# The first two batches' local softmax by head on ScalarE, the weights' pieces in six buffers, and a new hand-written order

## The chip, the cores and the metric

The kernel runs on one core of one Trainium2 chip. A core has five engines, each with an instruction queue of its own that is worked off in order: TensorE (PE in the profile, PEld its weight loads), VectorE (DVE), ScalarE (ACT), GpSimd (POOL) and SyncE (SP), which here only issues DMAs. The metric is the device time of one run in microseconds (us), the median of several runs. A profile is one execution taken apart instruction by instruction.

## The reference, cut to what matters

```python
# q, k, v: (B=8, H=8, S=576, D=64)
q_d, k_d, v_d = (mean of 4 neighbouring positions of q, k, v)       # 144 positions
out_d = softmax(q_d @ k_d.T / 8) @ v_d                             # "pooled" attention
out_up = repeat(out_d, 4, axis=position)
scores = where(|i - j| < 4, q @ k.T / 8, -1e9)                     # "local" attention
scores = scores - max(scores)
attn = exp(scores); attn = attn / (sum(attn) + 1e-9)
x = (out_up + attn @ v), as (4608 tokens, 512)
h = x @ w_in                                                       # (512, 1024)
e = exp(h - max(h)); solu = h * e / (sum(e) + 1e-9)
ln = (solu - mean) / sqrt(var + 1e-6) * g_ln
out = ln @ w_out                                                   # (1024, 512)
```

The weights `w_in` and `w_out` come as 64-bit floats, and the kernel makes 32-bit ones of them with integer operations.

## The kernel before, in words

**Attention, batch by batch.** A batch (`b` = 0 to 7) has 8 heads in 4 pairs (`pr`). For batches 0 to 2 TensorE transposes q and k (`qp_b_pr`, `kp_b_pr`, six transposes each), ScalarE copies them out of PSUM into `qT` and `kT`, and VectorE adds four neighbours each (`qd_flat`, `kd`). The pooled attention of a pair is `Pooled.steps`: scores `sd_b_pr` on PE, a maximum on DVE (`mxd`), three exponentials with their sums on ACT (`pd`, `smd`), a division on POOL, transposes `pdt` on PE, two copies `pdT` on ACT, and the product with the pooled values `vd` on PE (`po_b_pr`). The pooled values of batches 0 and 1 are made on PE (`pv_b_0`, `pv_b_1`) from the five value tiles `vw_b_u` and a matrix `sums`.

The local attention goes in five units (`u` = 0 to 4) of two windows of 64 positions each, `Local.by_tensor`: 16 small products give the scores `sc_b_u` of all heads; DVE adds the mask into `pl` (128 partitions by 4 pairs by 2 by 64) and takes each head's maximum `mxl`; POOL subtracts it; one ACT instruction takes the exponential of all 512 columns; DVE adds up each head (`sml`) and takes the reciprocal `rsl`; POOL multiplies; PE transposes (`plt_b_u`), ACT copies (`plT`), and 16 products with `vw` give `xp_b_u`, which is added to `x_b`. `pl` has four buffers, used in turn by unit number 5b + u.

**The feed-forward part** goes in 36 tiles of 128 tokens. `xhl(i)` splits x into two parts (`xh` on ACT, `xl` on POOL); `ffn_in` does 24 products of 128x512 into `h_i` and then the maximum `nmx` (DVE), `e` = exp (ACT), h times e (DVE), the mean's subtraction (ACT) and the squares' sum (ACT); `e` goes to DRAM as `u` and comes back as `v` (`ffn_back`), is transposed on DVE and split into `uh` (ACT) and `ul` (POOL); `ffn_out` does 24 products in two halves (first half columns 0 to 511 of the 1024, hence pieces 8 to 11 of the weights; second half pieces 12 to 15) into `o_i`.

**The weights** come in 16 pieces, 0 to 7 of `w_in`, 8 to 15 of `w_out`. `Weights.load(n)` loads piece n as 64-bit numbers, `Weights.f32` and `Weights.piece` make a 32-bit tile `w` of it and split it: one ACT instruction (L373), four on DVE (L375, L379, L384, L388), one or two on ACT (L407 for `w_out`, L409), one on POOL (L411). All eight pieces of `w_in` are needed before the first tile's products, all of `w_out` before the second half of `o_0`.

**The order** of all this is written out. `plan` collects the steps in program order, and `ORDER`, a string of 2072 numbers, gives the order in which they are issued; each engine keeps that order. `FILL` names PSUM tiles ahead of which PE does a number of products of the identity with itself (`idle_...`, L235), whose results nobody reads. A DMA that waits (for a buffer, or for the DMA eight before it) holds every DMA behind it in SP's queue.

Of the kernel before, what the change touches and what calls it, by code (L numbers as in the profile page):

```python
# [137 lines left out]
def pooled_local_attention_then_solu_ffn(  # L138
# [450 lines left out]

    ON_TENSOR = 8

    class Local:
# [514 lines left out]
```

## Time and profile before

| | |
|---|---|
| time, median of 3 runs | 617.78 us (616.66 to 618.25) |
| profiled execution | 620.24 us; span from first to last instruction 618.5 us |
| granted TensorE clock | 0.983 on average |
| busy | PE 597.7, DVE 394.0, ACT 374.1, POOL 374.6 us |
| DMA | 91.96 MB, 149 GB/s on average |
| longest chain | PE 81% of the span |

The span is the part of the time in which instructions ran; 1.7 us lie around it. PE's busy time holds the `idle_...` products too. From about 125 us on PE is busy without a gap worth speaking of; before that the batches 0 and 1, the weights and the first four tiles share the engines, and none of them is always busy.

### The profile page before, as it was taken

To read this page: it belongs to the slowest core of one execution; us is meant where nothing else is said; L and a number is where in the kernel's file an instruction comes from. 1 tells how busy PE (TensorE), PEld (TensorE's weight loads), DVE (VectorE), ACT (ScalarE), POOL (GpSimd) and SP (SyncE) were. 2 spreads that over 40 slices of the span, in tenths; PEclk is the share of its full clock that TensorE was granted. 3 is DMA by queue.
4 is the path that set the end of the run, shared out by engine and by line. 5 is a ranking of instruction groups with operands and counts; after the bars stand their busy time and mean duration, and the time that the engine had idled before them with its cause. 6 is when DMAs were issued, how large, how long until landed. Compare 5 with 4: busy or idle time off the path is not lost.

```text
span 618.5 us, 15210 instructions
## 1 busy us (share of the span) xinstructions
PE 597.7 (97%) x5912; PEld 470.4 (76%) x5912; DVE 394.0 (64%) x687; ACT 374.1 (60%) x810; POOL 374.6 (61%) x566
## 2 busy tenths in 40 slices
PE   5799998999999999999999999999999999999997
PEld 4686766878777777777777877777777777788876
DVE  4888897896646793668537873778367344443541
ACT  3647867965755576557755585557654675454451
POOL 7455485788735984499635983698556963332220
PEclk9698998999999999999999999999999999999999
DMA  9998966998795479535884398715532222234220
GB/s 179 216 208 204 186 163 183 182 163 195 187 204 149 133 191 193 153 115 159 185 179 131 109 192 195 198 43 164 164 115 81 92 87 86 86 107 147 86 103 34
DMA packets 205607, 91.96 MB, mean 149 GB/s; under 512 B 169568, under 2 KB 194400, under 8 KB 205536
## 3 DMA queue, kind: packets, MB, share of 16 engines
q1 hardware_dynamic: 205536, 91.00, 60.2%
q8 instruction: 46, 0.75, 0.5%
q14 instruction: 25, 0.20, 0.1%
HBM read 63.18 MB, written 27.79 MB: 147 GB/s over the span
## 4 chain that ended last, share of the span: by engine, by line
PE 81%; DVE 5%; ACT 5%; DMA 4%; SPq 3%; issue 1%; POOL 1%; ACTq 0%; DVEq 0%
PE o L965 32%; PE h L846 30%; PE xp L746 3%; PE plt L736 3%; PE po L828 3%; PE sc L696 3%; PE sd L772 2%; PE pdt L807 2%; DMA km<-in_k_dram 1%; SPq L550 1%; PE pv L488 1%; DMA w<-in_moe_w_in_dram 1%; SPq L314 1%; DVE pl L708 1%; ACT pd L787 1%
## 5 line engine op out<-in xcount | busy, mean ns | idle before, releaser
L846 PE MATMUL h<-wi_h,xh 128*128 128x512 f32 x288 | 117.4, 408 | 0.0
L965 PE MATMUL o<-wo_h,uh 128*128 128x512 f32 x288 | 117.0, 406 | 0.1
L965 PE MATMUL o<-wo_l,uh 128*128 128x512 f32 x288 | 114.2, 396 | 0.0
L846 PE MATMUL h<-wi_l,xh 128*128 128x512 f32 x288 | 114.1, 396 | 0.0
L846 PE MATMUL h<-wi_h,xl 128*128 128x512 f32 x288 | 114.0, 396 | 0.0
L951 POOL TENSOR_TENSOR ul<-v,uh 128x512 fp32r<-128x512 f32 x58 | 74.4, 1288 | 20.2 <-ACT uh L949 17.1
L854 DVE TENSOR_REDUCE nmx<-h 128x1 f32<-128x1024 f32 x36 | 43.7, 1215 | 61.9 <-PE h L846 61.9
L965 PE MATMUL o<-wo_h,ul 128*128 128x512 f32 x288 | 79.0, 396 | 0.0
L846 PEld LDWEIGHTS h<-wi_h,xh 128*128 128x128 f32 x288 | 54.2, 188 | 13.4 <-issue 0.4
L965 PEld LDWEIGHTS o<-wo_h,ul 128*128 128x128 f32 x288 | 54.2, 188 | 13.4
L965 PEld LDWEIGHTS o<-wo_h,uh 128*128 128x128 f32 x288 | 54.3, 189 | 13.3 <-ACT osb L972 0.3
L846 PEld LDWEIGHTS h<-wi_h,xl 128*128 128x128 f32 x288 | 54.2, 188 | 13.2
L846 PEld LDWEIGHTS h<-wi_l,xh 128*128 128x128 f32 x288 | 54.3, 189 | 11.6
L965 PEld LDWEIGHTS o<-wo_l,uh 128*128 128x128 f32 x288 | 54.2, 188 | 11.7
L999 POOL TENSOR_TENSOR xl<-x,xh 128x512 fp32r<-128x512 f32 (+1 forms) x40 | 47.3, 1191 | 25.2 <-ACT xh L996 25.1
L715 POOL TENSOR_TENSOR pl<-pl,mxl 128x512 f32<-128x512 f32 x40 | 42.8, 1075 | 26.7 <-DVE mxl L713 22.5
L858 ACT ACTIVATE e<-h,nmx 128x1024 f32<-128x1024 f32 x36 | 40.1, 1115 | 27.8 <-DVE nmx L854 27.5
L883 ACT ACTIVATE e<-e,nmu 128x1024 f32<-128x1024 f32 x35 | 40.2, 1149 | 25.2 <-POOL nmu L866 25.1
L943 DVE STREAM_TRANSPOSE v<-v 128x512 f32<-128x512 f32 x70 | 46.8, 693 | 12.8 <-DMA v<-u 12.5
L996 ACT ACTIVATE xh<-x 128x512 fp32r<-128x512 f32 (+1 forms) x40 | 22.7, 583 | 45.7 <-PE h L846 40.0
L949 ACT ACTIVATE uh<-v 128x512 fp32r<-128x512 f32 x70 | 43.3, 622 | 11.6 <-DVE v L943 5.7
L861 DVE SCALAR_TENSOR_TENSOR e<-h,e 128x1024 f32<-128x1024 f32 x36 | 43.5, 1210 | 10.2 <-ACT e L858 10.1
(121 smaller groups left out, 1150.3 us busy)
## 6 DMA issues: line engine op xcount, KB each, us to landing
u<-e SPq DMA_DIRECT2D x35, 512.0 KB
v<-u SPq DMA_DIRECT2D x140, 128.0 KB
vw<-in_v_dram SPq DMA_DIRECT2D x160, 64.0 KB
out_dram<-osb SPq DMA_DIRECT2D x36, 256.0 KB
vs<-in_v_dram SPq DMA_DIRECT2D x24, 288.0 KB
qm<-in_q_dram SPq DMA_DIRECT2D x20, 288.0 KB
km<-in_k_dram SPq DMA_DIRECT2D x20, 288.0 KB
w<-in_moe_w_out_dram SPq DMA_DIRECT2D x8, 512.0 KB
```

The lines of the kernel that those rows point to most:

```text
L715: nc.gpsimd.tensor_tensor(out=pl, in0=pl, in1=max_bc, op=ALU.subtract)
L846: nc.tensor.matmul(hps[:, n, :], src[:, cc, :], wt[:, cc, n * 512:(n + 1) * 512], start=(cc == 0 and src is xh and wt is wi_h), stop=(cc = ...
L854: nc.vector.tensor_reduce(out=nmx, in_=hf, op=ALU.max, axis=AX.X, negate=True)
L858: nc.scalar.activation(e, hf, AF.Exp, bias=nmx, scale=1.0, accum_out=se)
L861: nc.vector.scalar_tensor_tensor(out=e, in0=hf, scalar=1.0, in1=e, op0=ALU.mult, op1=ALU.mult, accum_out=su)
L883: nc.scalar.activation(e, e, AF.Identity, bias=nmu, scale=1.0)
L943: nc.vector.transpose(vg, vg)
L949: nc.scalar.activation(uh, tp, AF.Copy)
L951: (nc.vector if v is None or i in LATE else nc.gpsimd).tensor_tensor(out=ul, in0=tp, in1=uh.bitcast(F32), op=ALU.subtract)
L965: nc.tensor.matmul(o, src[:, j, :], wt[:, 4 * g + j, :], start=(g == 0 and j == 0 and src is uh and wt is wo_h), stop=(g == 1 and j == 3 a ...
L996: nc.scalar.activation(h, src, AF.Copy)
L999: nc.gpsimd.tensor_tensor(out=l, in0=src, in1=h.bitcast(F32), op=ALU.subtract)
```

## The change

Four things are edited. For batches 0 and 1 (`BY_HEAD = 2`) a local unit's exponential is no longer one ACT instruction behind a subtraction on POOL and ahead of a sum on DVE: DVE takes the negative maximum and scales it, and ACT does eight exponentials of 64 columns, one for each head, each with the head's maximum as bias and with its sum as a second output; DVE then adds 1e-9 to the eight sums. The raw 64-bit pieces 4, 5, 10 and 11 lie in the two buffers of `e` instead of in `big`; the 32-bit piece lies in turn in the buffers of `osb`, `uh` and `ul`, two each, instead of in the two of `osb`. `FILL` has other numbers (123 instead of 100 in all), and `ORDER` is another order of 2062 steps.

```diff
 FILL = {
-    "qp_0_3": (13, "o"), "pv_0_1": (8, "o"), "pdt_0_0": (3, "o"), "pdt_0_1": (1, "o"),
-    "sd_0_3": (2, "o"), "po_0_3": (3, "o"), "sc_0_0": (5, "o"), "plt_0_0": (12, "o"),
-    "xp_0_0": (2, "o"), "sc_0_1": (10, "o"), "h_0": (7, "o"), "qp_1_2": (3, "o"),
-    "po_1_3": (3, "h"), "kp_2_0": (5, "o"), "xp_2_0": (15, "h"), "o_34": (3, "h"),
-    "o_35": (5, "h"),
+    "qp_0_2": (4, "o"), "kp_0_2": (7, "o"), "qp_0_3": (3, "o"), "pv_0_0": (9, "o"),
+    "pv_0_1": (11, "o"), "po_0_0": (6, "o"), "sd_0_1": (4, "o"), "sc_0_0": (3, "o"),
+    "plt_0_0": (9, "o"), "sc_0_2": (17, "o"), "kp_1_1": (4, "o"), "sc_1_0": (8, "o"),
+    "sc_1_4": (2, "o"), "xp_1_4": (3, "o"), "qp_2_0": (5, "o"), "qp_2_2": (3, "o"),
+    "sc_2_1": (15, "h"), "o_34": (5, "h"), "o_35": (5, "h"),
 }
 ORDER = """
-0 33 7 14 1 2 3 28 8 4 5 6 9 10 135 40 11 12 29 13 15 41 42 50 143 16 43 51 44 151 136 52 137 45
...
+0 33 7 130 1 138 2 3 14 8 4 5 6 146 9 10 131 40 21 11 132 12 41 139 133 13 42 134 50 140 154 43
...
             elif n in (2, 3, 8, 9):
                 hl = moe.tile([P, DFF], F32, tag="v", name=f"w64_{n}", bufs=2)
+            elif n in (4,5,10,11):
+                hl = moe.tile([P, DFF], F32, tag="e", name=f"w64_{n}")
             else:
                 hl = big(f"w64_{n}")
...
-            t = moe.tile([P, DO], F32, tag="osb", name=f"w32_{n}", bufs=2)
+            t = moe.tile([P, DO], F32, tag=("osb", "uh", "ul")[n % 3], name=f"w32_{n}", bufs=2)
...
+    BY_HEAD = 2
...
+            if b < BY_HEAD:
+                nc.vector.tensor_reduce(out=mx, in_=pl, op=ALU.max, axis=AX.X, negate=True)
+                nc.vector.tensor_scalar(out=mx, in0=mx, scalar1=SCALE, scalar2=None, op0=ALU.mult)
+                yield
+                sm = small.tile([P, NPR, 2], F32, tag="sml", name=f"sml_{b}_{u}")
+                for pr in range(NPR):
+                    for a in range(2):
+                        nc.scalar.activation(
+                            pl[:, pr, a], pl[:, pr, a], AF.Exp, bias=mx[:, pr, a:a + 1], scale=SCALE,
+                            accum_out=sm[:, pr, a:a + 1],
+                        )
+                yield
+                nc.vector.tensor_scalar(out=sm, in0=sm, scalar1=1e-9, scalar2=None, op0=ALU.add)
+                rs = small.tile([P, NPR, 2], F32, tag="rsl", name=f"rsl_{b}_{u}")
+                nc.vector.reciprocal(out=rs, in_=sm)
+                yield
+            else:
...
-            row(it.steps(), 10 if isinstance(it, Pooled) else 11)
+            row(it.steps(), 10 if isinstance(it, Pooled) or bt.b < BY_HEAD else 11)
```

What the new order does is seen in the engines' queues. In the rows below the first number behind a name is the batch (or the piece, or the tile), the second the pair or unit, and the last a buffer's running number.

SP's queue near the start, before: `qm` and `km` are q and k, `w64` and `stage` the weights' pieces, `vw` the value tiles.

```order
L550 DMA km_0_125<-in_k_dram 96x6x64 x2
L314 DMA vw_0_0_188<-in_v_dram 64x4x64 x4
L360 DMA stage_211<-in_moe_w_in_dram 64x1024 x2
L314 DMA vw_0_1_223<-in_v_dram 64x4x64 x4
L360 DMA stage_211<-in_moe_w_in_dram 64x1024 x2
L360 DMA w64_2_260<-in_moe_w_in_dram 64x1024 x2
L360 DMA w64_3_291<-in_moe_w_in_dram 64x1024 x2
L360 DMA w64_4_304<-in_moe_w_in_dram 64x1024 x2
L550 DMA qm_0_3_313<-in_q_dram 96x6x64 x2
L550 DMA km_0_3_316<-in_k_dram 96x6x64 x2
L550 DMA qm_1_355<-in_q_dram 96x18x64 x2
L550 DMA km_1_356<-in_k_dram 96x18x64 x2
```

The same queue after:

```order
L362 DMA stage_166<-in_moe_w_in_dram 64x1024 x4
L552 DMA qm_0_124<-in_q_dram 96x6x64 x2
L552 DMA km_0_125<-in_k_dram 96x6x64 x2
L362 DMA w64_2_203<-in_moe_w_in_dram 64x1024 x2
L552 DMA qm_0_3_223<-in_q_dram 96x6x64 x2
L552 DMA km_0_3_226<-in_k_dram 96x6x64 x2
L362 DMA w64_3_259<-in_moe_w_in_dram 64x1024 x2
L362 DMA w64_4_287<-in_moe_w_in_dram 64x1024 x2
L314 DMA vw_0_0_314<-in_v_dram 64x4x64 x4
L314 DMA vw_0_1_369<-in_v_dram 64x4x64 x4
L314 DMA vw_0_2_442<-in_v_dram 64x4x64 x4
```

Pair 3's q and k of batch 0 now come behind three pieces of weights (0, 1 and 2) and no value tile, where they came behind five pieces and two value tiles; all five value tiles (`vw_0_3` and `vw_0_4` are the next rows) come ahead of batch 1's q and k, where three of them came behind these and behind pieces 5 to 7.

PE's queue ahead of the first tile's products, before:

```order
L746 MATMUL xp_0_0_937<-plT_0_0_615,vw_0_0_188 64x58 x16
L746 MATMUL xp_0_1_958<-plT_0_1_735,vw_0_1_223 64x58 x16
L736 MATMUL plt_0_2_978<-ident_82,pl_2_105 128x128 x4
L807 MATMUL pdt_1_0_991<-ident_82,pd_1_0_745 72x64 x12
L772 MATMUL sd_1_2_1008<-kd_1_619,qd_flat_111 64x144 x6
L736 MATMUL plt_0_3_1019<-ident_82,pl_3_106 128x128 x4
L235 MATMUL idle_h_0_1040<-ident_82 128x128 x7
L846 MATMUL h_0_1048<-wi_h_113,xh_0_1015 128x512
```

And after:

```order
L767 MATMUL xp_0_2_953<-plT_0_2_934,vw_0_2_442 64x58 x16
L570 MATMUL qp_1_3_981<-ident_82,qm_1_3_711 128x96 x6
L757 MATMUL plt_0_4_994<-ident_82,pl_0_103 128x128 x4
L570 MATMUL kp_1_3_1000<-ident_82,km_1_3_714 128x96 x6
L767 MATMUL xp_0_3_1011<-plT_0_3_988,vw_0_3_460 64x58 x16
L699 MATMUL sc_1_1_1033<-kT_1_779,qT_1_778 64x64 x16
L235 MATMUL idle_sc_1_0_1062<-ident_82 128x128 x8
L699 MATMUL sc_1_0_1071<-kT_1_779,qT_1_778 64x64 x16
L793 MATMUL sd_1_0_1088<-kd_1_780,qd_flat_111 64x144 x6
L867 MATMUL h_0_1097<-wi_h_113,xh_0_971 128x512
```

Before the first tile starts, batch 0's local units 0 to 3 are now done to the end (only `xp_0_4` is left) and batch 1's transposes of q and k come late, just ahead of it; before, units 2 to 4 were open and batch 1's pooled pairs further on.

ScalarE's queue there, after (a unit's eight exponentials are one row with x8):

```order
L411 ACTIVATE wi_h_113<-w32_7_900 128x4x4x32
L375 ACTIVATE w32_11_1059<-w64_11_822 128x512
L724 ACTIVATE pl_2_105,sml_1_1_1112<-pl_2_105,mxl_1_1_1055 128x64 x8
L804 ACTIVATE mxd_1_0_1110<-mxd_1_0_1110 128x3
L808 ACTIVATE pd_1_0_1131,smd_1_0_1132<-sd_1_0_1088,mxd_1_0_1110 128x144 x3
L812 ACTIVATE smd_1_0_1132<-smd_1_0_1132 128x3
L724 ACTIVATE pl_1_104,sml_1_0_1174<-pl_1_104,mxl_1_0_1122 128x64 x8
```

`wi_h` from piece 7, the last of `w_in`, stands there ahead of batch 1's first exponentials; five pieces of `w_out` have had their first step (L375) by then and wait for the rest.

From `h_4` on PE's queue is the same in both kernels, row for row but for the `idle_...` ones, and ahead of `h_4` PE does the same products in both, in another order.

More of the change, by code (lines that the diff above doesn't have):

```diff
@@ L712, in by_tensor @@
             yield
-            nc.vector.tensor_reduce(out=mx, in_=pl, op=ALU.max, axis=AX.X)
-            yield
-            nc.gpsimd.tensor_tensor(out=pl, in0=pl, in1=max_bc, op=ALU.subtract)
-            yield
-            nc.scalar.activation(by_pair, by_pair, AF.Exp, scale=SCALE)
-            yield
-            sm = small.tile([P, NPR, 2], F32, tag="sml", name=f"sml_{b}_{u}")
-            nc.vector.tensor_reduce(
-                out=sm, in_=pl_all.rearrange("p (r a w) -> p r a w", r=NPR, a=2), op=ALU.add, axis=AX.X
-            )
-            rs = small.tile([P, NPR, 2], F32, tag="rsl", name=f"rsl_{b}_{u}")
-            nc.vector.reciprocal(out=rs, in_=sm)
-            yield
+            if b < BY_HEAD:
[15 more added lines that the diff above has]
+            else:
+                nc.vector.tensor_reduce(out=mx, in_=pl, op=ALU.max, axis=AX.X)
+                yield
+                nc.gpsimd.tensor_tensor(out=pl, in0=pl, in1=max_bc, op=ALU.subtract)
+                yield
+                nc.scalar.activation(by_pair, by_pair, AF.Exp, scale=SCALE)
+                yield
+                sm = small.tile([P, NPR, 2], F32, tag="sml", name=f"sml_{b}_{u}")
+                nc.vector.tensor_reduce(
+                    out=sm, in_=pl_all.rearrange("p (r a w) -> p r a w", r=NPR, a=2), op=ALU.add, axis=AX.X
+                )
+                rs = small.tile([P, NPR, 2], F32, tag="rsl", name=f"rsl_{b}_{u}")
+                nc.vector.reciprocal(out=rs, in_=sm)
+                yield
             nc.gpsimd.tensor_tensor(
```

192 rows, old and new, of the table ORDER are left out of this document.

## The prediction

> **What bounds the kernel now.** I read the busy time by stage first, cut where the first tile's products start, where the first output tile `o_0` starts, and near `h_4` (the columns: stretch, its length, busy us of PE, PEld, DVE, ACT, POOL, granted clock, DMA share, GB/s), and then what lies in the early stages at 15 us each.
>
> ```profile
> 0.00:24.00 24.00, 15.41 (x113) 12.19 (x114) 13.63 (x29) 12.28 (x32) 14.30 (x43) 0.85 1.00 197
> 24.00:72.50 48.50, 44.17 (x615) 36.81 (x613) 41.88 (x71) 31.81 (x80) 26.88 (x23) 0.90 1.03 207
> 72.50:124.40 51.90, 49.27 (x694) 37.69 (x692) 44.76 (x72) 39.83 (x74) 33.71 (x43) 0.97 0.74 172
> 124.40:147.10 22.70, 22.70 (x285) 18.62 (x282) 16.19 (x31) 12.95 (x29) 19.82 (x24) 1.00 0.86 169
> 147.10:618.50 471.40, 466.11 (x4217) 365.09 (x4215) 277.55 (x488) 277.27 (x597) 279.84 (x436) 1.00 0.52 137
> ```
>
> ```profile
> 60.00:75.00 15.00, 14.59 (x243) 11.85 (x242) 13.32 (x21) 14.50 (x40) 8.85 (x8) 1.00 0.96 170
> 105.00:120.00 15.00, 14.93 (x192) 12.80 (x191) 13.09 (x24) 14.22 (x27) 10.60 (x15) 1.00 0.80 174
> ```
>
> From 147.1 us PE is busy 466.11 of 471.40 us and bounds the kernel. Since PE's rows from `h_4` on are the same after the change, the question is only when `h_4` starts. Ahead of it PE's busy time is partly the identity products, so I asked for line L235 alone (columns: stretch, length, PE, PEld, clock, DMA share, GB/s), then for PE in order of time.
>
> ```profile
> 0.00:72.50 72.50, 21.86 (x138) 20.06 (x138) 0.88 1.02 203
> 72.50:124.40 51.90, 1.58 (x13) 1.28 (x11) 0.97 0.74 172
> 124.40:147.10 22.70, 4.55 (x36) 4.17 (x36) 1.00 0.86 169
> ```
>
> ```profile
> 30.20 0.85 PE L568 MATMUL kp<-ident,km 96*128 96x96 f32 x6 [2.03 <-DMA km<-in_k_dram]
> ...
> 33.16 1.98 PE L696 MATMUL sc<-kT,qT 64*64 64x64 f32 x96
> ...
> 61.25 0.71 PE L828 MATMUL po<-pdT,vd 72*64 72x144 f32 x8 [0.27 <-DVE vd L502]
> ...
> 72.53 0.48 PE L846 MATMUL h<-wi_h,xh 128*128 128x512 f32 x1
> 72.84 0.40 PE L846 MATMUL h<-wi_l,xh 128*128 128x512 f32 x1
> 73.08 0.40 PE L846 MATMUL h<-wi_h,xl 128*128 128x512 f32 x1
> ...
> 124.37 0.50 PE L965 MATMUL o<-wo_h,uh 128*128 128x512 f32 x1
> ...
> 141.81 3.62 PE L235 MATMUL idle_xp<-ident 128*128 128x128 f32 x30
> ...
> 146.87 0.48 PE L846 MATMUL h<-wi_h,xh 128*128 128x512 f32 x1
> ```
>
> `h_4` starts at 146.87. Up to there PE idles 8.59 + 4.33 + 2.63 = 15.55 us (length less busy) and spends 21.86 + 1.58 + 4.55 = 27.99 us on identity products, so 146.87 - 15.55 - 27.99 = 103.3 us are work that the change leaves as it is. Those 43.5 us are all that there is to win. They come from three things: data that land late (the DMA engines are full, share 1.00 and 1.03, up to the first tile), the chain of batch 0 through the values, and the weights' pieces on ACT and DVE.
>
> **The change part by part.** *Loads.* The last transposes of batch 0, `kp_0_3`, wait for k until 30.20. What lies ahead in SP's queue is counted in KB of the DMAs:
>
> ```profile
> vw<-in_v_dram SPq DMA_DIRECT2D x46, 64.0 KB
> stage<-in_moe_w_in_dram SPq DMA_DIRECT2D x8, 256.0 KB
> w<-in_moe_w_in_dram SPq DMA_DIRECT2D x8, 256.0 KB
> qm<-in_q_dram SPq DMA_DIRECT2D x12, 144.0 KB
> km<-in_k_dram SPq DMA_DIRECT2D x12, 144.0 KB
> ...
> 39.91 9.12 SPq L314 DMA_DIRECT2D vw<-in_v_dram  x12
> ```
>
> Before: 16 of q and k (2304 KB), 10 of weights (2560), 8 of values (512), 5376 KB. After: 2304 + 6 of weights (1536) = 3840. The 1536 KB less (1.57 MB) are 7.8 us at about 202 GB/s: k lands at 22.4. The last values were issued at 39.91 + 9.12 = 49.0; now 3840 + 1024 + 1280 = 6144 KB (6.29 MB) must pass: 31 us, with 2.5 at the start some 34. Batch 1's q and k land later, about 44, and nobody is ready for them sooner. So the scores start at about 24.5 instead of 33.16.
>
> *Exponentials.* ACT's nearest rows are the pooled ones, 144 columns with a sum, and the unit's exponential that goes away (its shape's group):
>
> ```profile
> 12.20 0.38 ACT L787 ACTIVATE pd<-sd,mxd 128x144 f32<-128x144 f32 x1
> 12.48 0.19 ACT L787 ACTIVATION_READ_ACCUMULATOR pd<-sd,mxd 128x1 f32 x1
> 12.57 0.37 ACT L787 ACTIVATE pd<-sd,mxd 128x144 f32<-128x144 f32 x1
> ...
> L858 ACT ACTIVATE e<-h,nmx 128x1024 f32<-128x1024 f32 x4 | 4.4, 1108 | 0.0
> L717 ACT ACTIVATE pl<-pl 128x512 f32<-128x512 f32 x10 | 6.1, 622 | 2.2 <-POOL pl L715 2.2
> ```
>
> One starts 0.37 after the last, sum included. For 64 columns I take 0.29, since 80 columns less are 0.08 at the 0.95 ns a column between 512 columns (0.622) and 1024 (1.108); bounds 0.19 (the sum's row alone) and 0.37. Eight are 2.3 us, against 0.52 for the old one (0.62 less the 0.10 by which the next may start earlier, 12.48 for 12.20 + 0.38): +1.8 a unit, +17.8 for ten (10 to 24). The Trainium skill, page "ScalarE: Activation LUTs", section "Rules for kernel authors", budgets about 0.3 us for each ACTIVATE and 0.83 ns a column. By that eight would take an estimated 2.8 us, and batch 1's five units 1.5 us more than my sum has, the result 614.5 instead. The trace is against it: 144 columns would take 0.42 by the page, and start 0.37 apart.
>
> What leaves the other engines, and what the piece's first step waited for:
>
> ```profile
> L720 DVE TENSOR_REDUCE sml<-pl 128x8 f32<-128x520 f32 x10 | 6.8, 677 | 0.2 <-ACT pl L717 0.2
> L375 DVE TENSOR_SCALAR w<-w 128x512 f32<-128x512 f32 x16 | 11.1, 694 | 4.6 <-ACT w L373 4.6
> L724 DVE RECIPROCAL rsl<-sml 128x8 f32<-128x8 f32 x10 | 2.0, 203 | 0.9 <-POOL pl L715 0.5
> L715 POOL TENSOR_TENSOR pl<-pl,mxl 128x512 f32<-128x512 f32 x10 | 11.5, 1163 | 10.4 <-DVE mxl L713 10.4
> L373 ACT ACTIVATE w<-w 128x512 f32<-128x512 f32 x12 | 8.1, 677 | 1.1 <-DMA w<-in_moe_w_in_dram 0.7 <-POOL wi_l L411 0.3
> ACT w L407 <- DVE w L388: 6.1, 4, 3.9
> ```
>
> DVE loses ten sums (about 6 us) and gains twenty tiny ones of the reciprocals' shape (0.1 to 0.2 each): -3 (-2 to -4). POOL loses 11.5 us, and waited more than that, so it is worth nothing by itself; DVE's piece instructions may run a little sooner beside a quieter POOL (0 to 2 us of DVE, 0 taken). A unit's own chain is no shorter: the subtraction and the sum go, eight exponentials come. The buffers: ACT waited 0.3 us for a piece's buffer (`POOL wi_l` above), so six instead of two are worth 0 to 0.3 by themselves; what they allow is to order the first steps early, which spares ACT some of the 6.1 us behind DVE.
>
> *Order, up to the first tile.* I walked PE's and ACT's rows side by side. With scores at 24.5, DVE's mask and maximum are done at about 28 and ACT begins the exponentials. From there to `wi_h` of piece 7 and the next row ACT has 31.7 us of work by its own rows (five units 11.5, eight first steps 4.6, 16 copies of q, k and `po` and transposes 10, the rest 5.6): 59.7 if it never waits. It waits some 7 us around the values: 52 identity products at 0.24 us (the row at 141.81 has 30 records, two a product, up to the next start) stand between `sc_0_1` and `po_0_0`, which comes at 45 to 49 instead of 61.25. ACT's 15.4 us from there to batch 1's last copy of k give 64.7, and two scores, 8 identity products and `sd_1_0` put the first tile at 68.4, against 72.53, with PE 0.6 us of work further on (`xp_0_2`, `xp_0_3`, `plt_0_4`, `sc_1_1` done, `sd_1_1`, `sd_1_2`, `pdt_1_0` not). ACT cannot do better than 62; at the 66% of the old stage (31.81 of 48.50) it would be 76.
>
> *From there to `h_4`.* The second half of `o_0` needs the last piece: ACT has 55.1 us from the first tile to that piece's `wo_h` (batch 1's exponentials 11.5, `w_out` 11.7, the first four tiles 13, pooled pairs 8, copies 11), where the old stage had 41. PE has 58, DVE 45. ACT's share in the old stage was 39.83 of 51.90; it reached 14.50 and 14.22 of 15.00 in the two 15 us rows. I take 90%, because now its queue is full of work that is ready, and every step of tile and attention passes it: 61.2, and 1.3 for POOL's last split: 68.4 + 62.5 = 130.9. Then half of `o_0`, `o_1` and three small steps up to `h_4`, 10.7 us: 141.6, against 146.87. Gain 5.3. The check on PE's side: 103.3 + 113 identity products (26.8) + idle = 141.6 leaves 11.5 us of idling, 4 less than before, 4.4 of them the start.
>
> *Behind `h_4`.* Two identity products more ahead of `o_34`: 0 to 0.5, 0.5 taken. The earlier tail of loads meets DMA engines that were at 0.52. **Sum:** -4.8. The profiled execution took 620.24, 2.46 above the median 617.78; less 4.8 it would be 615.4, and the median 613.0.
>
> **The rivals.** (1) *ACT becomes the bound: slower.* It was on the chain already at 60 to 75 us. If between the first tile and the last piece it is busy only the old stage's 79% (41 of 51.9 by the same rows), the 55.1 us take 69.7, `o_0`'s second half starts at 139.4, `h_4` at 150.1: +3.2, and 0.5: 621.5. The gain is gone at 83%. For it: ACT gets 14 us more in a stage where DVE (44.76 of 51.90) and PE were nearly full too. Against it: the 6.1 us behind DVE become fewer. (2) *The early lead is given back.* Data land early, but the last pieces of `w_out` are now issued by SP behind batch 3's q and k and the first `u`, and set `o_0`; ACT at 81 to 86%: 616 to 619.6. (3) *PE itself sets the end.* All other queues keep up, PE idles only 8 us at the start: 103.3 + 26.8 + 8 = 138, 609.4. (4) *The change does not do what it says*: ACT still takes the pieces late and the buffers bring nothing; then only the loads' 8 us count, most of which the pieces' chain swallows, a case of (2).
>
> **How the numbers follow.** Forecast 613.0, chance 0.5, its own range 610.5 to 616; (1) 0.2; (2) with (4) 0.22; (3) 0.08. A measurement of this kernel tells about 0.3% (1.9 us) from no change. Faster 0.58, same 0.22, slower 0.20. The range of 609 to 621 reaches (3) and the middle of (1).
>
> **What would show it.** k of pair 3 landing near 22, scores at 24 to 25, `po_0_0` before 50, the first tile at 66 to 71, ACT at 88% or more from there to the last `wo_h`, `h_4` at 140 to 144, eight exponentials 0.29 apart. It is wrong if `h_4` starts after 147, if exponentials start 0.37 apart, or if PE waits anew behind 150.

## The result and the profile after

The changed kernel takes 624.92 us (median of 4 runs, 622.87 to 627.79), the kernel before beside it 618.01 (616.66 to 620.56): 1.010 times as long, with a 95% interval of 1.0063 to 1.0137. The forecast was 613.0, in a range of 609 to 621. The profiled execution took 624.20 us with a span of 622.5, against 620.24 and 618.5 before. That is only 4.0 us apart, since the profiled execution of before was 2.2 us slower than its median and this one 0.7 faster than its own.

PE in order of time, for the places that the prediction named:

```profile
22.61 0.66 PE L570 MATMUL kp<-ident,km 96*128 96x96 f32 x6
...
23.89 0.69 PE L699 MATMUL sc<-kT,qT 64*64 64x64 f32 x32
...
49.40 0.71 PE L849 MATMUL po<-pdT,vd 72*64 72x144 f32 x8
...
69.95 0.50 PE L867 MATMUL h<-wi_h,xh 128*128 128x512 f32 x1
...
126.33 0.40 PE L986 MATMUL o<-wo_h,uh 128*128 128x512 f32 x1
...
138.49 0.50 PE L986 MATMUL o<-wo_h,uh 128*128 128x512 f32 x1
...
149.73 0.48 PE L867 MATMUL h<-wi_h,xh 128*128 128x512 f32 x1
```

k of pair 3, the scores, `po_0_0` and the first tile `h_0` are where they were forecast. The rest is not: the second half of `o_0` starts at 138.49 and `h_4` at 149.73, 2.9 us later than before. The stages show where (the same columns as before: length, busy us of PE, PEld, DVE, ACT, POOL, clock, DMA share, GB/s):

```profile
0.00:24.00 24.00, 17.47 (x143) 14.88 (x147) 16.08 (x29) 13.43 (x34) 16.87 (x44) 1.00 1.05 205
24.00:69.90 45.90, 40.77 (x684) 33.84 (x684) 34.77 (x66) 38.02 (x137) 18.42 (x15) 1.00 0.94 200
69.90:126.30 56.40, 51.26 (x600) 39.14 (x599) 44.96 (x83) 49.37 (x165) 24.15 (x31) 0.94 0.78 172
126.30:138.40 12.10, 11.82 (x211) 10.11 (x209) 11.83 (x19) 10.41 (x20) 7.40 (x11) 1.00 0.40 106
138.40:149.70 11.30, 10.95 (x120) 8.54 (x111) 7.38 (x16) 7.38 (x14) 11.30 (x13) 1.00 0.79 192
149.70:622.50 472.80, 466.74 (x4223) 365.71 (x4221) 277.49 (x488) 274.78 (x594) 285.15 (x445) 1.00 0.53 137
```

From `h_0` to `h_4` it is 79.8 us, where it was 74.3; ahead of `h_0` 2.6 us were won, behind `h_4` 1.1 lost. In the slow stage ACT is busy 49.37 of 56.40 us. And it is mostly ACT for which PE waits there, 4.2 of 5.2 us (PE's waits from 69.95 to 138.4: us, times, longest):

```profile
PE kp L570 <- ACT kT L576: 1.9, 1, 1.9
PE plt L757 <- ACT plT L760: 1.1, 1, 1.1
PE plt L757 <- POOL pl L747: 1.0, 1, 1.0
PE xp L767 <- ACT plT L760: 0.6, 1, 0.6
PE xp L767 <- ACT pdT L838: 0.3, 1, 0.3
PE sc L699 <- ACT kT L576: 0.3, 1, 0.3
```

Ahead of the first two waits stands a block of ACT's queue with the sixteen exponentials of two units of batch 1, 89.1 to 94.5 us; the copies `kT` and `plT` come behind it. A unit's exponentials in ACT's order of time:

```profile
69.75 0.35 ACT L724 ACTIVATE pl<-pl,mxl 128x64 f32<-128x64 f32 x1 [0.86 <-DVE mxl L719]
70.00 0.19 ACT L724 ACTIVATION_READ_ACCUMULATOR pl<-pl,mxl 128x1 f32 x1
70.09 0.34 ACT L724 ACTIVATE pl<-pl,mxl 128x64 f32<-128x64 f32 x1
...
72.09 0.33 ACT L724 ACTIVATE pl<-pl,mxl 128x64 f32<-128x64 f32 x1
```

From 69.75 to 72.09 are seven steps: 0.334 us each, so eight take 2.67 us for the 0.52 of the one instruction, 2.15 more a unit.

### The profile page after: what moved, and what is told of

Read it like the earlier page. It is cut to its first block, busy times and chain, and to the rows that moved or that the text cites. A ratio compares the mean times of both kernels' runs of the same rounds, so it can differ in the third digit from the quotient of the medians.

```text
span 622.5 us, 15466 instructions
## 1 busy us (share of the span) xinstructions
PE 599.0 (96%) x5958; PEld 472.2 (76%) x5958; DVE 392.5 (63%) x697; ACT 393.4 (63%) x960; POOL 363.3 (58%) x556
## 4 chain that ended last, share of the span: by engine, by line
PE 76%; ACT 8%; DVE 4%; DMA 2%; SPq 1%; issue 1%; POOL 1%; POOLq 0%; DVEq 0%; ACTq 0%
PE o L986 30%; PE h L867 28%; PE plt L757 3%; PE xp L767 3%; PE sc L699 3%; PE po L849 3%; ACT pl L724 2%; PE sd L793 2%; PE pdt L828 2%; DMA v<-u 1%; PE pv L490 1%; DVE nmx L875 1%; PE idle_sc L235 1%; DMA u<-e 1%; ACT qT L576 1%
## 5 line engine op out<-in xcount | busy, mean ns | idle before, releaser
L972 POOL TENSOR_TENSOR ul<-v,uh 128x512 fp32r<-128x512 f32 x58 | 74.3, 1291 | 16.6 <-ACT uh L970 14.1
L747 POOL TENSOR_TENSOR pl<-pl,rsl 128x512 f32<-128x512 f32 x40 | 41.9, 1051 | 31.2 <-DVE rsl L731 14.3
```

What stands on the lines that cost most here:

```text
L747: nc.gpsimd.tensor_tensor(out=pl, in0=pl, in1=rs.unsqueeze(3).broadcast_to([P, NPR, 2, W]), op=ALU.mult)
L972: (nc.vector if v is None or i in LATE else nc.gpsimd).tensor_tensor(out=ul, in0=tp, in1=uh.bitcast(F32), op=ALU.subtract)
```

## The experiments

The theory to test ("ScalarE theory") is that these exponentials fill ScalarE's queue and that this alone loses the time. The rival ("order theory") is that the new order is slower whatever the exponentials cost. All times are medians, and each ratio is against runs of the kernel before taken beside them on the same chip (medians 618.6 to 619.8 us).

**One exponential again, in the new order** (e1). GpSimd's subtraction comes back in the step of the maximum, VectorE's sum in the step of the reciprocal:

```diff
-                for pr in range(NPR):
-                    for a in range(2):
-                        nc.scalar.activation(pl[:, pr, a], ..., bias=mx[...], accum_out=sm[...])
+                nc.scalar.activation(by_pair, by_pair, AF.Exp, scale=SCALE)
```

> The changed kernel with its order, identity products and buffers, but the ten local units of batches 0 and 1 take their exponentials in one instruction of 512 columns again (GpSimd subtracts the maximum in the step of the maximum, VectorE sums in the step of the reciprocal). ScalarE theory (the eight exponentials, 2.67 us a unit for 0.52, filled ScalarE's queue in the early stages; 21 us come off it): h_4 at 138 to 143 for 149.7, 612 to 617 us. Order theory (the new order itself is later, since the last pieces of w_out and their first steps stand behind u of tile 0 in SP's queue and late on ScalarE): h_4 stays at 148 to 151, 621 to 626 us.

625.08 us, ratio 1.0094 (1.0063 to 1.0126): the order theory's number. But this run gives back three things at once: ScalarE is light, and GpSimd and VectorE have their work again.

**One maximum a row** (e2): no subtraction on GpSimd, and one exponential.

```diff
+                nc.vector.tensor_reduce(out=top, in_=by_pair, op=ALU.max, axis=AX.XY, negate=True)
...
+                nc.scalar.activation(by_pair, by_pair, AF.Exp, bias=top, scale=SCALE)
```

> As the first, but the unit's exponential has one bias for each row, the maximum over all eight heads, so GpSimd subtracts nothing and ScalarE has one instruction (the softmax is the same as long as the heads' maxima are not far apart). ScalarE theory: as the first or up to 2 us better, because 1.16 us of GpSimd and a hop leave each unit's chain: 610 to 616 us. Order theory: 621 to 626 us. A third theory, that GpSimd's subtractions are what the old kernel lost time by, has this one at least 3 us under the first.

620.78 us, 1.0025 (0.9999 to 1.0050): 4.3 us below e1, as the third theory had it. It lies well above the 610 to 616 of the ScalarE theory and just below the 621 to 626 of the order theory.

**One instruction, all else as after the change** (e9): the clean test of ScalarE, since VectorE and GpSimd keep the work that they have after the change. One head's maximum and one sum stand in for all eight, so the weights are not those of the reference.

```diff
-                        nc.scalar.activation(pl[:, pr, a], ..., accum_out=sm[:, pr, a:a + 1])   # eight times
+                nc.scalar.activation(by_pair, by_pair, AF.Exp, bias=mx[:, 0, 0:1], scale=SCALE, accum_out=s1)
```

> The changed kernel with one exponential of 512 columns in place of the eight, with one bias (head 0's maximum) and one accumulator that stands in for all eight sums: the weights of the local attention in batches 0 and 1 are not those of the reference. VectorE and GpSimd do what they do after the change, ScalarE does some 20 us less. ScalarE theory (the eight exponentials alone cost what the new order loses against the one with the row maximum, and more since VectorE's ten sums are away too): h_0 to h_4 in 72 to 75 us, 615 to 620 us. Theory that the order loses the time in any case: 621.5 to 625 us.

619.24 us, 0.9999 (0.9976 to 1.0023). Seven exponentials a unit fewer are worth 5.7 us, and with them gone the new order is level with the kernel before. But e1 has them gone too and is 5.8 us slower than e9: GpSimd's subtraction and VectorE's sum cost as much there, 4.3 of it the subtraction (e1 less e2). So in the new order the eight exponentials and what they replaced cost the same. The stage from `h_0` to `o_0` of four kernels in the new order, in which PE has the same 600 records (after, e1, e2, e9):

```profile
69.95:126.33 56.38, 51.24 (x600) 39.14 (x599) 44.99 (x83) 49.35 (x165) 24.18 (x31) 0.94 0.78 172
```

```profile
73.74:125.28 51.54, 48.52 (x600) 37.41 (x599) 48.19 (x79) 38.87 (x90) 29.92 (x37) 1.00 0.70 146
```

```profile
74.43:124.72 50.29, 48.30 (x600) 37.23 (x599) 46.49 (x83) 39.31 (x90) 24.95 (x32) 1.00 0.75 152
```

```profile
72.06:121.80 49.74, 48.03 (x600) 37.34 (x599) 44.29 (x83) 40.02 (x95) 24.77 (x32) 1.00 0.74 154
```

With ScalarE at 39 to 40 us the stage takes 50 to 51.5, with 49.35 it takes 56.4. Of the 6.6 us between the first row and the last, 3.2 are the same 600 records at a lower granted clock (51.24 us at 0.94, 48.03 at 1.00), and 3.4 are PE's idle time (5.14 for 1.71). The stage is not the whole time, though: e1's is short too, but there `h_0` comes at 73.74, and from `o_0` to `h_4` it takes 25.21 us where the changed kernel took 23.40.

**Batch by batch** (e7, e8): batch 0 head by head, batch 1 as in e1, or as in e2.

```diff
+    ONE = (1,)          # e7; e8: ROW = (1,)
...
+            if b in ONE:     # one exponential of 512 columns
...
+            elif b < BY_HEAD:
```

> The changed kernel, but only batch 0 takes its exponentials head by head; batch 1 has one instruction of 512 columns with GpSimd's subtraction in the step of the maximum. Stage theory (head by head helps up to the first tile, where h_0 came at 70 for 73.7, and hurts from there to h_4, 79.8 us for 76.8): 70 + 76.8 = 146.8, 620 to 623 us. Theory that the two ways are worth the same everywhere: 624 to 626 us.

> As the run before, but batch 1 has the one maximum a row. Stage theory: h_0 at 70, then the 73.7 us of the run with the row maximum: h_4 at 143.7, 616 to 619.5 us. Theory that up to h_0 the clock and not the exponentials made the difference: 619.5 to 622 us.

624.78 us (1.0097, 1.0062 to 1.0132) and 620.72 (1.0035, 1.0005 to 1.0066): the times of e1 and e2. How batch 0 takes its exponentials makes no difference that these runs can tell; `h_0` was at 73.5 in both, though every instruction up to batch 1's first maximum is that of the changed kernel, where it was at 69.95. In e17 below, which differs from the changed kernel only behind `h_0`, it was at 73.35. PE's clock is what differs, behind a wait for `qT` of 0.4 us in the changed kernel and 2.1 in e17 (50 to 60 and 60 to 70 us, after and e17):

```profile
50.00:60.00 10.00, 8.49 (x152) 6.82 (x150) 5.91 (x12) 9.68 (x31) 3.39 (x3) 1.00 1.09 285
60.00:70.00 10.00, 9.32 (x229) 7.89 (x219) 9.47 (x15) 9.14 (x18) 5.12 (x4) 1.00 1.03 228
```

```profile
50.00:60.00 10.00, 7.44 (x72) 5.89 (x67) 4.76 (x10) 8.05 (x29) 1.71 (x3) 0.80 1.09 269
60.00:70.00 10.00, 8.72 (x194) 7.57 (x197) 7.64 (x12) 7.85 (x16) 4.12 (x4) 0.86 0.82 204
```

Some 3.4 us of clock are missing in the second pair. So those 69.95 us were a lucky execution, and my stage theory, which had added up stages of single executions, fell.

**The old order** (e3: head by head; e5: one maximum a row; the step of the subtraction stays empty in both. e4: the buffers alone).

```diff
+                nc.vector.tensor_scalar(out=mx, in0=mx, scalar1=SCALE, scalar2=None, op0=ALU.mult)
+                yield
+                yield
```

> The kernel before, its order, identity products and buffers, but batches 0 and 1 take exponentials head by head (the step of the subtraction is left empty). ScalarE theory: 21 us more on ScalarE; 31.8 + 10.7 us in the 48.5 before the first tile still fit (88%), 39.7 + 10.7 in the 51.8 from there to o_0 do not, at the 87% that ScalarE reached after the change they take 58: h_4 at 150 to 154, 621 to 626 us. Order theory: the exponentials are hidden, 617 to 619.5 us.

> The kernel before with its order, identity products and buffers, but batches 0 and 1 take one maximum for each row over all heads as the exponential's bias: GpSimd's subtraction (11.5 us for ten units) is gone and ScalarE still has one instruction a unit. Chain theory (what the early stages lose is a unit's chain, of which the subtraction's 1.16 us go, ten times, partly behind other work): 612 to 617 us. ScalarE theory alone (its queue had room in the old order): ScalarE waited 3.3 us for subtractions there, so at most 3 us: 616 to 619 us.

629.72 us (1.0168, 1.0131 to 1.0206) and 618.31 (0.9990, 0.9965 to 1.0014). In the old order the eight exponentials cost 10.7 us, over half of it ahead of `h_0` (at 78.20): my expectation, which had hidden the first half, was too low. e5 is where the ScalarE theory alone had it, at 616 to 619. The new order thus does make room for them: like for like, against one maximum a row, they cost 11.4 us in the old order (e3 less e5) and 4.1 in the new (the changed kernel less e2). What it does not do is gain anything when they are gone.

```diff
-            t = moe.tile([P, DO], F32, tag="osb", name=f"w32_{n}", bufs=2)
+            t = moe.tile([P, DO], F32, tag=("osb", "uh", "ul")[n % 3], name=f"w32_{n}", bufs=2)
+            elif n in (4, 5, 10, 11):
+                hl = moe.tile([P, DFF], F32, tag="e", name=f"w64_{n}")
```

> The kernel before with only the buffers changed: raw pieces 4, 5, 10, 11 in the buffers of e, the 32-bit pieces in six buffers. ScalarE theory: 617 to 619 us, h_4 within 1 us of 146.9, since ScalarE waited 0.3 us for a buffer. Rival: the buffers themselves cost, because e, uh and ul of the first tiles now wait for pieces: h_4 over 148, 620 us or more.

631.08 us, 1.0192 (1.0153 to 1.0230): the rival, and more. SP's longest wait of the first 150 us, and PE's:

```profile
SPq L362 <- DVE w L390: 11.7, 2, 11.3
```

```profile
PE qp L570 <- DMA qm<-in_q_dram: 9.4, 4, 4.2
```

The load of piece 11 now waits 11.3 us for the buffer of `e` that piece 5 holds until its last step on VectorE (L390), and behind it in SP's queue wait q and k, for which PE then idles. In the old order, then, the new buffers cost 12 us; the new order without them was not tried.

**Waits moved out of the way, in the new order.** In e2 ScalarE's first step of piece 6 waited 3.7 us for its DMA, ahead of the copy of q that PE needed. First comes the same kernel again (e10, with nothing moved), then two moves in `ORDER`, with the row maximum (e11) and with the eight exponentials (e12).

> A second look at the kernel with one maximum a row in the new order, for the spread of its early waits: if the wait of ScalarE's first step of piece 6 for its DMA (3.7 us at 51 us, with PE at half clock for some 10 us behind it) belongs to the order, it stands there again, h_0 at 73 to 75; if it was chance, h_0 is at 69 to 71.

> The row maximum in the new order, with two moves in the order: the first five steps of piece 6 stand behind the copy of q of batch 1's first pair (ScalarE waited 3.7 us for piece 6's DMA ahead of that copy, PE idled and fell to half clock), and tile 2's transposes on VectorE with their copies stand behind the sum of batch 2's unit 1 (VectorE waited there for v, and PE for that unit, in two runs). Order theory (waits placed ahead of ready work lose the time): h_0 at 69 to 71, 613 to 618 us. Rival, the pieces of w_in only get later by it and h_0 stays: 619 to 622 us.

> The changed kernel, eight exponentials and all, with the same two moves in the order. Order theory: 619 to 622.5 us. ScalarE theory (the queue is full from h_0 on, what is won before it is lost behind it): 623 to 626 us.

In e10 the wait was there again (3.3 us, `h_0` at 74.95; one run of 623.53 us). Moved, it was gone and `h_0` came at 70.33, yet `h_4` at 146.47, and the time was 619.44 us (1.0011, 0.9988 to 1.0033): the lead was lost again behind `h_0`. With the eight exponentials it became 629.26 us (1.0161, 1.0133 to 1.0189), slower than both theories had it; why is open.

**Is VectorE the next bound?** (e13 with the row maximum, e14 with the eight exponentials, e15 in the kernel before): the clamp of the pieces of `w_out` is left out.

```diff
-            nc.vector.tensor_scalar(out=t, in0=t, scalar1=F64_LO, scalar2=F64_HI, ...)
+            if n < 2 * NCC:
+                nc.vector.tensor_scalar(out=t, in0=t, scalar1=F64_LO, scalar2=F64_HI, ...)
```

> The row maximum in the new order, and VectorE leaves out the clamp of the eight pieces of w_out (8 of its 0.69 us instructions, 5.5 us; values outside the range of a 32-bit float are then not bounded). Theory that VectorE is the next bound of the new order once ScalarE is free (it was busy 46.5 of the 50.3 us from h_0 to o_0): 3 to 5 us less than the 620.8 of the row maximum, 615.5 to 618 us. Theory that what stands behind it is GpSimd and the way of v (PE waited 2.3 us for them ahead of h_4): 619 to 621 us.

> The changed kernel, eight exponentials and all, without the same clamps. ScalarE theory: ScalarE's queue is the bound there, 5.5 us off VectorE change little: 623 to 625.5 us. Theory that ScalarE and VectorE hold each other up equally: 620 to 622.5 us.

> The kernel before without the same clamps, for comparison: what VectorE's 5.5 us are worth in the old order (VectorE busy 44.7 of 51.8 us from h_0 to o_0). If both orders are bound by VectorE: 614 to 616.5 us. If the old order is not: 617.5 to 619.5 us.

621.19, 626.49 and 619.13 us (1.0018, 0.9993 to 1.0043; 1.0123, 1.0092 to 1.0155; 0.9994, 0.9972 to 1.0016). VectorE's 5.5 us are worth nothing anywhere (e14 even lies above both of its forecasts), so it is not the bound, in spite of 46.5 busy us of 50.3 in e2.

**Are the identity products in the way?** (e6: none ahead of `h_4`; e16, e17: none between `h_0` and `h_4`, with the row maximum and its moves, and in the changed kernel; e18: the row maximum in the old order without the 23 ahead of `po_1_3`, `kp_2_0` and `xp_2_0`.) The edit of e17, which e16 has too:

```diff
-    "sc_1_4": (2, "o"), "xp_1_4": (3, "o"), "qp_2_0": (5, "o"), "qp_2_2": (3, "o"),
-    "sc_2_1": (15, "h"), "o_34": (5, "h"), "o_35": (5, "h"),
+    "o_34": (5, "h"), "o_35": (5, "h"),
```

> The changed kernel without the identity products ahead of h_4 (113 of 123 left out). Theory that they are in the way (31.3 us of PE's time ahead of h_4 for 28.0 before, which is the whole loss): 617 to 622 us. ScalarE theory (PE waits for ScalarE there anyway, they fill the waits): 623 to 627 us, with PE's idle time ahead of h_4 grown from 17 to some 45 us. A third, that they hold the clock: more stretches at half clock, 628 us or more.

> The row maximum in the new order with its two moves, and without the 28 identity products that stand between h_0 and h_4 (7.4 us of PE, which there was busy 71.1 of 76.1 us). Theory that PE itself is the bound of that stage once ScalarE is light, and the identity products are in its way: h_4 5 to 7 us earlier, 612 to 615.5 us. Theory that they fill waits: the same idle time opens in their place, 618 to 621 us.

> The changed kernel without the same 28 identity products. ScalarE theory: it is bound there by ScalarE, PE idles in their place, 623.5 to 626 us; if PE also falls to half clock in the opened gaps, up to 628. Theory that they cost it 7 us: 617 to 620 us.

> The row maximum in the old order without the 23 identity products of po_1_3, kp_2_0 and xp_2_0 (some 6 us of PE ahead of h_4). If they are in the way there: 612 to 615 us. If they fill waits: 617 to 619.5 us, and more where PE falls to half clock.

626.23 us (1.0134, 1.0095 to 1.0173), 620.80 (1.0029, 1.0010 to 1.0047), 626.64 (1.0132, 1.0110 to 1.0153) and 617.76 (0.9982, 0.9959 to 1.0005). They fill waits: from `h_0` to `h_4` PE with them (e11) and without (e16):

```profile
70.33:146.47 76.14, 71.06 (x919) 55.91 (x917) 67.13 (x119) 57.39 (x122) 43.46 (x53) 1.00 0.75 170
```

```profile
72.31:148.64 76.33, 65.83 (x862) 50.46 (x861) 67.40 (x119) 57.02 (x122) 43.59 (x53) 0.98 0.75 172
```

5.2 busy us fewer, and the stage as long as it was.

No version beat the kernel before by more than its interval; e18 and e5 come nearest.

## Why the prediction was wrong

*The exponentials* had the right mechanism at too low a price: 0.334 us apart, within my bounds of 0.19 to 0.37 but not the 0.29 that I took, +21.5 us for ten units by their spacing instead of +17.8. I had taken 80 columns' worth of time off the pooled instruction's 0.37 at the slope between 512 and 1024 columns; the two instructions with a sum show that most of the 0.37 does not depend on the columns. The Trainium skill, page "ScalarE: Activation LUTs", section "Rules for kernel authors", gave an estimated 2.8 us a unit where I had 2.3: measured 2.67, nearer to the page. (The 1.5 us and 614.5 that I put beside it are a slip: five units at 2.8 for 2.3 are 2.5 us, and 615.5.) VectorE lost 1.5 us instead of 3, because the new scaling of eight maxima takes 0.316 us on average (0.17 to 0.66), not 0.1 to 0.2. POOL's 11.5 were right: 374.55 less 363.30 is 11.25. That they are worth nothing by themselves held in the old order (e5 less the kernel before: -0.4 us) but not in the new one, where the subtraction cost 4.3 (e1 less e2).

*The stage from the first tile to the last `wo_h`* is the step that failed:

```profile
69.95:137.00 67.05, 61.63 (x772) 47.97 (x771) 55.40 (x99) 58.32 (x181) 30.15 (x40) 0.95 0.71 161
```

I had 55.1 us of ACT at a 90% share, 61.2 us. It was 58.32 us at 87%: 67.05, 5.85 more. Of the 3.2 us of work 1.8 are the dearer exponentials (40 by 0.044). Then came the first tile 1.55 later than forecast, and 0.7 more behind the last `wo_h`: together 8.1, which is 149.7 for 141.6. This is rival (1), ScalarE as the bound, which had put `h_4` at 150.1 and the time at 621.5 at a chance of 0.20; it came with more work and a higher share than I had given it. e9 shows that it is ScalarE's work that counts: 5.7 us of the time go with it. PE's clock, for which I had no term in this stage, is about half of what e9 wins back in it (3.2 of 6.6 us above).

*PE's side* adds up the same way: idle 17.4 us instead of 11.5, identity products 31.3 instead of 26.8 (the first eight took 2.07 us for four, later ones 1.16), other work 101.0 instead of 103.3.

*The loads.* k and the scores came as forecast, but the byte count hid a second effect. SP's queue, before and after:

```profile
33.31 2.63 SPq L360 DMA_DIRECT2D w<-in_moe_w_in_dram  x2
36.05 3.81 SPq L360 DMA_DIRECT2D stage<-in_moe_w_in_dram  x4
39.91 9.12 SPq L314 DMA_DIRECT2D vw<-in_v_dram  x12
```

```profile
20.34 14.82 SPq L314 DMA_DIRECT2D vw<-in_v_dram  x20
35.20 1.25 SPq L362 DMA_DIRECT2D w<-in_moe_w_in_dram  x2
36.58 2.08 SPq L552 DMA_DIRECT2D qm<-in_q_dram  x2
38.76 6.39 SPq L552 DMA_DIRECT2D km<-in_k_dram  x2
45.26 3.87 SPq L362 DMA_DIRECT2D stage<-in_moe_w_in_dram  x4
```

The twenty small value DMAs now go in one row, and SP needs 0.74 us for each. While it issues them the DMA engines are no longer full (20 to 36 us, before and after):

```profile
20.00:36.00 16.00, 13.51 (x176) 12.32 (x174) 13.00 (x20) 7.23 (x18) 4.87 (x4) 0.67 1.14 215
```

```profile
20.00:36.00 16.00, 16.00 (x237) 14.57 (x237) 14.20 (x27) 11.99 (x47) 7.82 (x6) 1.00 0.67 141
```

74 GB/s less over 16 us are 1.2 MB, some 5.8 us of the full engines, and pieces 6 and 7 of `w_in`, without which no tile starts, are issued at 45.26 instead of 36.05. That fits with an early start of the scores that buys no early tile: in the other profiles of the new order with its identity products `h_0` came at 70.3 to 75.0, in those of the old order and its buffers with light exponentials at 70.8 to 74.5. I had costed this step by bytes alone, and the 4.1 us that it was to win at `h_0` are not there. Values in fewer and larger DMAs were not tried, so this link is read from the traces and not shown by a run. The one test near it is mixed: with ScalarE's step for piece 6 moved out of the way `h_0` came at 70.33 in e11, but at 74.63 in e12.

*Rival (2)* was seen in part: the last pieces of `w_out` (13 and 14, then 15) are issued behind batch 3's q and k, where 14 and 15 had been at 89.77:

```profile
94.42 6.54 SPq L294 DMA_DIRECT2D qm<-in_q_dram  x4
101.06 5.87 SPq L294 DMA_DIRECT2D km<-in_k_dram  x4
106.97 1.86 SPq L362 DMA_DIRECT2D w<-in_moe_w_out_dram  x2
...
117.96 0.55 SPq L362 DMA_DIRECT2D w<-in_moe_w_out_dram  x1
```

But in e9 the same late pieces gave the time of before, so they did not decide by themselves.

*Behind `h_4`* I had 0.5; it was 1.1, within what two executions differ by.

What stays open is why the new order gains nothing even with ScalarE light. Taking 5.5 us from VectorE, 5 us from PE, or the early waits away changed nothing that these runs can tell; other waits stood in their place (in e13, for one, PE waited 1.6 us for POOL's `pl` and 1.3 for DVE's `e`). No single engine was shown to hold it.

## What to carry to other kernels

Price a small instruction by the distance between the starts of two of its kind with the same outputs, and do not read the bound off an engine's share alone: ScalarE's 87% of a stage cost 5.7 us, while VectorE's 92% (46.49 of 50.29 us in e2) cost nothing. Only work taken off one engine at a time told the two apart. When transfers are moved in a queue, count the queue's time to issue them beside their bytes. And where several engines stand near the limit, a change of one of them is worth only what the next wait leaves: a version with one part undone says more than the sum of the parts.

## What the runs showed of the hardware

A value DMA of 64 KB took SP 0.74 us to issue (20 in 14.82, of which 0.6 us are waits for earlier loads), and while SP issued a row of them the 16 DMA engines were at a share of 0.67.

PE's clock fell to half behind two waits of 1.9 and 1.1 us (after, the columns as above):

```profile
93.18:96.96 3.78, 0.71 (x6) 0.56 (x7) 3.18 (x6) 3.75 (x14) 0.87 (x2) 0.89 0.96 208
96.96:102.96 6.00, 6.00 (x62) 4.10 (x64) 2.67 (x6) 5.26 (x15) 1.97 (x3) 0.50 1.02 161
```

PE worked 0.71 of 3.78 us and then ran at half clock for more than 6 us, though busy without a gap. The Trainium skill, page "TensorE: Matmul & The Clock Gate", section "What's actually happening", has the clock halved after at least one idle window of about 3.4 us and back after at least one busy one of the same length. The trace agrees only in part: PE was not idle throughout ahead of the half clock, and this one lasted nearly two such windows. Without identity products the mean clock of e6's runs fell to 0.952 to 0.981, and the median was 1.3 us from that of the changed kernel, whose own runs spread over 5. That does not price the lower clock by itself, since e6 also spares PE the products.
